# Group 2 of an attention and FFN kernel: all five chunks of the next x turned by DMA, and six weight units split again on the spot

## The chip, the cores and the metric

One core of a Trainium2 chip. The metric is the device time of one execution in microseconds, the median of several runs. TensorE (PE) multiplies, VectorE (DVE), ScalarE (ACT) and GpSimd (POOL) work element by element, and SyncE (SP) mostly issues DMAs.

## The reference

```python
x = A_x                                  # [1, 2048, 640]
xn = layernorm(x)
q, k, v = split(xn @ A_wqkv)             # 32 heads of 20
s = local_attention(q, k, v) @ A_wo      # window of 8 keys, every 2nd row back
g = silu(silu(xn @ B_w1) @ B_w2)         # the FFN: 640 -> 1536 -> 640
out = x + s * g
```

All data are float32.

## The kernel before

**Precision.** A float32 operand is split in a high part (rounded to the fast matmul type by a copy, `hi`) and a low part (value minus high part, `lo`). Each product is three matmuls: high by high, low by high, high by low. So every weight block and every activation needs a high part, made by ScalarE, and a low part, made by VectorE.

**Groups.** The 2048 rows form four groups of 512 (four tiles of 128). For each group the kernel does the QKV product in four quarters of the columns, q = 0 to 3, and then the FFN, while VectorE does the attention. With the FFN of group g goes the output projection (`wo`) of group g - 1, and the preparation of group g + 1's x.

**The FFN's order** (`STEPS`). An "up" unit f makes 128 of the 1536 hidden columns (w1); a "down" unit f multiplies them with 128 rows of w2. In group 2: up 0, five `wo` units, up 1, 2, down 0, 1, 2, up 3, 4, 5, down 3, 4, 5, up 6, 7, 8, down 6, 7, 8, up 9, 10, 11, down 9, 10, 11. After an up unit ScalarE applies SiLU twice (`sh`, the high part, and `sf`, the whole), VectorE subtracts (`sl`). Up units alternate between two PSUM banks (`rot`), `sh` and `sl` have three buffers each, `sf` has one. At the end ScalarE moves the six output banks (`acc`) to G (`gate`).

**Weights.** Each of the units takes the next of seven slots (`w`, numbered 75 to 81 in the rows below), so a slot comes free when the unit seven before is done. A unit met for the first time comes raw over SP's queue into a staging buffer (`xr`, three of them), is split by ScalarE and VectorE, and both halves are stored to memory (`half_w`). Every later time POOL loads the halves, 640 KB, with no splitting.

**The next x.** The normalised rows of group g + 1 stand in XIN. They must be turned: columns become partitions, in five chunks of 128 columns. There are two ways. On TensorE (`split_t`): four transposes into a bank, from which ScalarE writes the high part (`th`) and a whole copy, and VectorE the low part (`tl`). By DMA (`turn_x`): ScalarE separates the 16-bit halves of a chunk into a buffer (`send`, 128x1024), SP issues two DMA transposes, ScalarE puts the halves together again (`join`) and makes the high part, VectorE the low part. The buffers are five pieces of G and TURN, so G must have been read out by the output rows of group g - 1 (`xr<-xr,gate` on POOL) before. Chunks 3 and 4 use as their first buffer what chunks 0 and 1 landed in.

**The order.** All engines but TensorE get their order from a planner (class `Weave`): operations carry a duration and a priority, the planner runs them against its own model of the engines and the DMA, adds dependencies where it sees TensorE wait, and writes them out. `at` is the earliest time of a send or join. Each engine then runs its list in order. A DMA transpose is given 1.27 us a half by size and `SLOW` = 8 us more until it lands; the model knows nothing of a load standing behind a transpose in the queue.

Of the kernel before, what the change touches and what calls it, by code (L numbers as in the profile page):

```python
# [8 lines left out]
F32 = mybir.dt.float32  # L9
# [6 lines left out]
P = 128  # L16
# [7 lines left out]
T = 4  # L24
# [34 lines left out]
O_BACK = (), (80.0, 82.0), (80.0, 82.0), (40.0, 55.0, 60.0)  # L59
X_BY = {1: 2, 3: 0, 4: 1}  # L60
SLOW, ISSUE, SUB_LATE = 8, 2.0, 3
PACE0, PACE = -20.0, 12.0
BACK = {1: 0.0, 2: 40.0}
QAT = 48
OAT = 16
STORE_Q = 1, 3
SHARED = (1, 0), (1, 2), (2, 0), (2, 2), (3, 0)
X_AT = 1.2, 6, 8
# [255 lines left out]
def local_attention_silu_ffn(ctx: ExitStack, tc: tile.TileContext, x, wqkv, wo, w1, w2, out):  # L324
# [152 lines left out]
    def store_at(u):  # L477

        return 1 + (u[0] == "wo" or u[0] == "q" and u[2] in STORE_Q)
# [20 lines left out]
    def raw_tile(k):  # L500
# [7 lines left out]
        return "xr", k % 3  # L508

    def raw_load(k):  # L510
# [12 lines left out]
        pairs = []  # L523
        if u[0] == "q":
            _, q, c = u
            whole = wqkv[c * P:(c + 1) * P, :]
            pairs.append((r.rearrange("p (k m) -> p k m", k=3), whole.rearrange("p (k m) -> p k m", k=3)[:, :, q * CQ:(q + 1) * CQ]))
        elif u[0] == "w1":
            pairs.append((r.rearrange("p (c f) -> p c f", c=DC),
                          w1.rearrange("(c p) f -> p c f", p=P)[:, :, u[1] * P:(u[1] + 1) * P]))  # L530
        else:
            m = wo if u[0] == "wo" else w2
            pairs.append((r, m[u[1] * P:(u[1] + 1) * P, :]))
        by = nc.scalar if k in BY_ACT else nc.sync

        def go():
            for to, frm in pairs:
                by.dma_start(to, frm)
        if k in BY_ACT:
            add("ACT", 0.65 * len(pairs), go, [], kr, -1, nbytes=n * P * 4)  # L540
            return
        dma(go, [], kr, n * P * 4, 1 + k if k < 2 * DC else clock[0] + 5, (0.62 if k < 2 * DC else 0.45) * len(pairs))

    def raws_due(i, k):

        while rawn[0] < len(fresh) and fresh[rawn[0]] <= i + RAW_AHEAD and raw_in.get(raw_tile(rawn[0]), -1) <= k:
            raw_load(rawn[0])
            rawn[0] += 1

    def w_load():  # L550
# [10 lines left out]
        kh, kl = ("wh", s), ("wl", s)  # L561
        due = clock[0]
        if what[i] == "load":
# [16 lines left out]
        if what[i] == "store":  # L580
            kept = dram.tile([P, 2, n], F32, name="half_" + "_".join(map(str, u)))
            halves[u] = kept
            dma(lambda: nc.sync.dma_start(kept, both.bitcast(F32)), [kh, kl], [("half", u)], 2 * n * P * 4, due + 25)
        raws_due(i, k)
# [95 lines left out]
    def turn_x(c, i, by, to, at, back):  # L680
# [3 lines left out]
             (chunk_span("x", c, True), chunk_span("x", c)))  # L684

    def turn_o(c, i, by, to, at, back):
        qs = range(c * P // CQ, ((c + 1) * P - 1) // CQ + 1)
        send(O, c, [("o", q, t) for q in qs for t in (0, 2)], "o", by, to, at)
        join(to, by[0].rearrange("p (t n) -> p t n", t=T), both(by[1]), [], c, i, (OH, OL), back)

    def turn_os(g, i, begun):
# [254 lines left out]
    def qkv_phase(g, i, io):  # L946
        for q in range(NQ):
            if g == 0 and q == 0:
                ps = first_quarter(i)
            else:  # L950
                ps = [bank() for t in range(T)]
                for c in range(DC):
# [12 lines left out]
                    if g:  # L965
                        for k in O_AT.get((q, c), ()):
                            if k not in O_DMA.get(g - 1, ()):
                                o_chunk(g - 1, k, io)
# [212 lines left out]
    def ffn_phase(g, i, ix, io):  # L1181
# [12 lines left out]
        by_dma = X_DMA.get(g, ())  # L1194
        bufs = [("buf", c, h) for c in range(DC) for h in range(2)]
# [29 lines left out]
        if g < NG - 1:  # L1225
            turn_os(g, i, begun)

    add("POOL", 0.7, consts, [], ["consts"], 0)
# [38 lines left out]
```

## Time and profile before

| | |
|---|---|
| median of 3 runs | 598.78 us (598.73 to 599.15) |
| the profiled execution's own time | 598.41 us |
| its span | 596.3 us |
| TensorE clock | 0.999 |
| TensorE busy | 590.6 us, 99% |
| VectorE busy | 513.3 us, 86% |
| ScalarE busy | 248.7 us, 42% |
| POOL busy | 168.2 us, 28% |
| moved by DMA | 164.21 MB, mean 275 GB/s |

Times below are microseconds from the span's start. A row of the timeline gives start, duration, engine, line, operation, output<-input, shape and count, and in brackets the idle time of the engine before it and what ended it. A row of the windows gives the stretch, its length, busy time of PE, PEld (weight load into TensorE), DVE, ACT and POOL with counts, the granted clock, the DMA share and GB/s. A row of groups gives count, then busy time and mean ns, then idle time and what ended it.

### The profile page before, as it was taken

Reading aid. Unit: us, or ns where it says so; the run is one execution under the profiler, and the core shown is the slowest. Engines: PE = TensorE matmul, PEld = TensorE weight load, DVE = VectorE, ACT = ScalarE, POOL = GpSimd, SP = SyncE. Lnnn points to the kernel's source line nnn. Section 1 sums busy time; section 2 is a strip of 40 time slices with the busy share of each in tenths; the row PEclk is TensorE's granted clock in tenths of the full one; section 3 lists DMA queues with packets and bytes.
Section 4 is the critical chain, followed back from the end, with each engine's and each line's share of the span. In section 5 each row is a group of like instructions: output and inputs, shape, how many; then the busy total and the mean of one; then the engine's idle time right before and its main releaser. Section 6 shows DMA issues by size and latency. Waiting matters only on the chain.

```text
span 596.3 us, 9080 instructions
## 1 busy us (share of the span) xinstructions
PE 590.6 (99%) x3443; PEld 555.9 (93%) x3443; DVE 513.3 (86%) x505; ACT 248.7 (42%) x444; POOL 168.2 (28%) x229
## 2 busy tenths in 40 slices
PE   8999999999999999999999999999999999999997
PEld 7999999999999999999999999999999999999997
DVE  6499999999799978999988996999838799998744
ACT  5437375452545223747523604443412333335230
POOL 5800102233110153442221126543121233434100
PEclk9999999999999999999999999999999999999999
DMA  9999999879999999999699999998689999797952
GB/s 295 311 295 334 296 411 402 322 252 300 271 316 326 313 257 324 239 202 239 191 319 306 303 346 304 263 208 286 211 220 283 294 320 295 227 203 215 241 185 89
DMA packets 80263, 164.21 MB, mean 275 GB/s; under 512 B 19949, under 2 KB 44237, under 8 KB 80221
## 3 DMA queue, kind: packets, MB, share of 16 engines
q1 hardware_dynamic: 60381, 83.93, 52.1%
q0 software_dynamic: 19296, 79.31, 46.5%
q8 instruction: 27, 0.44, 0.3%
q10 hardware_dynamic: 544, 0.41, 0.2%
q14 instruction: 15, 0.12, 0.1%
HBM read 107.91 MB, written 34.16 MB: 238 GB/s over the span
## 4 chain that ended last, share of the span: by engine, by line
PE 98%; DMA 0%; DVE 0%; issue 0%
PE acc L1005 23%; PE acc L1007 15%; PE acc L960 10%; PE acc L961 10%; PE acc L962 10%; PE rot L1140 9%; PE rot L1142 9%; PE rot L1141 9%; PE acc L910 2%; PE rot L629 1%; DMA xin<-in_A_x_dram 0%; PE rot L894 0%; PE rot L1123 0%; DVE st L879 0%; PE rot L853 0%; DVE gate L1091 0%
## 5 line engine op out<-in xcount | busy, mean ns | idle before, releaser
L960 PE MATMUL acc<-w,th 128*128 128x480 f32 x300 | 110.6, 369 | 0.0
L961 PE MATMUL acc<-w,tl 128*128 128x480 f32 x300 | 109.8, 366 | 0.0
L962 PE MATMUL acc<-w,th 128*128 128x480 f32 x300 | 109.8, 366 | 0.0
L1005 PE MATMUL acc<-w,sh 128*128 128x384 f32 x384 | 108.6, 328 | 0.0
L1007 PE MATMUL acc<-w,sh 128*128 128x256 f32 x384 | 104.7, 273 | 0.0
L754 DVE TENSOR_TENSOR pr<-q,kv 128x2560 f32<-128x2560 f32 x32 | 90.2, 2819 | 15.9 <-DMA kv<-carry 12.7
L796 DVE TENSOR_TENSOR pr<-q,kv 128x2560 f32<-128x2560 f32 x32 | 91.5, 2860 | 1.4 <-DVE l L757 0.5
L1140 PE MATMUL rot<-th,w 128*128 128x512 f32 x240 | 91.8, 383 | 0.0
L1141 PE MATMUL rot<-tl,w 128*128 128x512 f32 x240 | 91.0, 379 | 0.0
L1142 PE MATMUL rot<-th,w 128*128 128x512 f32 x240 | 91.0, 379 | 0.0
L757 DVE TENSOR_REDUCE l<-pr 128x128 f32<-128x2560 f32 x32 | 89.7, 2804 | 0.2
L1153 ACT ACTIVATE sh<-rot 128x512 fp32r<-128x512 f32 x48 | 28.8, 599 | 134.2 <-PE rot L1142 134.1
L565 POOL DMA_DIRECT2D w<-half_w x72 | 39.0, 542 | 156.6 <-PE acc L1007 57.6
L1007 PEld LDWEIGHTS acc<-w,sh 128*128 128x128 f32 x384 | 73.7, 192 | 0.6
L1005 PEld LDWEIGHTS acc<-w,sh 128*128 128x128 f32 x384 | 72.6, 189 | 0.6
L565 POOL DMA_DIRECT2D w<-half_q x52 | 28.0, 538 | 119.8 <-PE acc L962 74.3
L962 PEld LDWEIGHTS acc<-w,th 128*128 128x128 f32 x300 | 56.7, 189 | 4.0
L960 PEld LDWEIGHTS acc<-w,th 128*128 128x128 f32 x300 | 56.7, 189 | 3.9
L961 PEld LDWEIGHTS acc<-w,tl 128*128 128x128 f32 x300 | 56.7, 189 | 3.9
L1005 PE MATMUL acc<-w,sl 128*128 128x384 f32 x192 | 55.9, 328 | 0.0
L1155 DVE TENSOR_TENSOR sl<-sf,sh 128x512 fp32r<-128x512 f32 x48 | 39.3, 819 | 16.8 <-ACT sf L1154 16.8
L1007 PE MATMUL acc<-w,sl 128*128 128x256 f32 x192 | 52.3, 273 | 0.0
(110 smaller groups left out, 1070.0 us busy)
## 6 DMA issues: line engine op xcount, KB each, us to landing
w<-half_w POOLq DMA_DIRECT2D x72, 640.0 KB, 7.0
w<-half_q POOLq DMA_DIRECT2D x52, 480.0 KB, 5.8
half_w<-w SPq DMA_DIRECT2D x24, 640.0 KB
half_q<-w SPq DMA_DIRECT2D x20, 480.0 KB
kv<-kv SPq DMA_DIRECT2D x15, 560.0 KB
w<-half_wo POOLq DMA_DIRECT2D x10, 640.0 KB, 5.6
kv<-kv SPq DMA_DIRECT2D x15, 420.0 KB
gate<-in_B_w_dram SPq DMA_DIRECT2D x16, 320.0 KB
```

Of the source, the lines that this page charges most:

```text
L565: add("POOL", 1.0, lambda: nc.gpsimd.dma_start(both, src), [("half", u)], [kh, kl], due + 10, nbytes=2 * n * P * 4)
L754: dve(2560, lambda: nc.vector.tensor_tensor(out=PR, in0=win(qq[:, t:t + 2, :], W, 0), in1=win(kv[:, 0, t:t + 2, :], W, CQ), op=OP.mult), h ...
L757: dve(2560, lambda: nc.vector.tensor_reduce(out=l[:, t:t + 2].rearrange("p t w h -> p (t w h)"), in_=PR.rearrange("p t w (h d) -> p (t w h ...
L796: dve(2560, lambda: nc.vector.tensor_tensor(out=PR.rearrange("p t w (h d) -> p t (w h) d", d=DH), in0=e[:, t:t + 2].rearrange("p t w h -> ...
L960: nc.tensor.matmul(o, hi, vh, start=c == 0, stop=False)
L961: nc.tensor.matmul(o, lo, vh, start=False, stop=False)
L962: nc.tensor.matmul(o, hi, vl, start=False, stop=c == DC - 1)
L1005: nc.tensor.matmul(a[t][0][:, :CA].rearrange("p (m h) -> p m h", h=2), st, col_a(w), start=first, stop=last)
L1007: nc.tensor.matmul(b[t // 2][0][:, h * CB:(h + 1) * CB].rearrange("p (m h) -> p m h", h=2), st, col_b(w), start=first and h == 0, stop=las ...
L1140: nc.tensor.matmul(to, wh[:, cs], hi, start=c == 0, stop=False)
L1141: nc.tensor.matmul(to, wh[:, cs], lo, start=False, stop=False)
L1142: nc.tensor.matmul(to, wl[:, cs], hi, start=False, stop=c == DC - 1)
```

## The change

In group 2's FFN, chunks 0 and 1 of group 3's x are turned by DMA too, as 2, 3 and 4 were; the sends are asked for 4, 16, 28, 40 and 52 us after `wo`. In the same FFN the w2 units 6 to 11, which POOL loaded as stored halves, come raw again over SP's queue, at most six units ahead, and are split by ScalarE and VectorE. Their halves from the first group stay stored for groups 1 and 3. The rest of the diff (a helper `raw_ap`, empty tables `O_HOME` and `STORE_W2`, a way to turn group 0's x) does nothing with these tables.

```diff
-X_DMA = {1: (0, 1, 2, 3, 4), 2: (2, 3, 4)}
+X_DMA = {1: (0, 1, 2, 3, 4), 2: (0, 1, 2, 3, 4)}
...
-PACE0, PACE = -20.0, 12.0
+PACE0 = {1: -20.0, 2: 4.0}
+PACE = 12.0
...
+RAW_AGAIN = {("w2", 3): [(f,) for f in range(6, 12)]}
+AGAIN_AHEAD = 6
...
-        what.append("load" if n > at else "store" if n == at and n < again[u] else "split")
+        what.append("load" if n > at and u[1:] not in RAW_AGAIN.get((u[0], n), ()) else "store" if n == at and n < again[u] else "split")
...
+    def ahead(i):
+        return AGAIN_AHEAD if units[i][0] == "w2" and i > fresh[early] else RAW_AHEAD
+
     def raws_due(i, k):
 
-        while rawn[0] < len(fresh) and fresh[rawn[0]] <= i + RAW_AHEAD and raw_in.get(raw_tile(rawn[0]), -1) <= k:
+        while rawn[0] < len(fresh) and fresh[rawn[0]] <= i + ahead(fresh[rawn[0]]) and raw_in.get(raw_tile(rawn[0]), -1) <= k:
...
-                    turn_x(c, ix, by, (piece(G, c), ("buf", c)), clock[0] + PACE0 + PACE * k, clock[0] + BACK[g])
+                    turn_x(c, ix, by, (piece(G, c), ("buf", c)), clock[0] + PACE0[g] + PACE * k, clock[0] + BACK[g])
```

TensorE's list loses two entries of four transposes. The other lists move.

SP's list in group 2's FFN, before: from the first output row of group 1 to the last transposes (`xr` are output rows here).

```order
L1056 DMA out_0_dram<-xr1_108 128x640
L1056 DMA out_0_dram<-xr2_109 128x640
L1056 DMA out_0_dram<-xr0_107 128x640
L662 DMA_TRANSPOSE gate_106<-turn_112 128x4x128 x2
L1053 DMA xr1_108<-in_A_x_dram 128x640
L1056 DMA out_0_dram<-xr1_108 128x640
L662 DMA_TRANSPOSE gate_106<-gate_106 128x4x128 x4
```

SP's list at the same place, after, from the first transposes on (`xr<-in_B_w2` are raw rows of units 6 to 11, in this order).

```order
L676 DMA_TRANSPOSE gate_106<-turn_112 128x4x128 x2
L1090 DMA out_0_dram<-xr0_107 128x640
L1087 DMA xr1_108<-in_A_x_dram 128x640
L545 DMA xr2_109<-in_B_w2_dram 128x640
L676 DMA_TRANSPOSE gate_106<-gate_106 128x4x128 x2
L545 DMA xr0_107<-in_B_w2_dram 128x640
L1090 DMA out_0_dram<-xr1_108 128x640
L545 DMA xr1_108<-in_B_w2_dram 128x640
L545 DMA xr2_109<-in_B_w2_dram 128x640
L676 DMA_TRANSPOSE gate_106<-turn_112 128x4x128 x2
L545 DMA xr0_107<-in_B_w2_dram 128x640
L676 DMA_TRANSPOSE gate_106<-gate_106 128x4x128 x2
```

Behind the last of these follow the raw rows of unit 11 (`xr1_108`) and chunk 4's two transposes. Five pairs of transposes now alternate with the raw rows, one queue for all.

ScalarE's list, before, from up unit 8's activations (`sh2_86`) to up unit 10's (`sh1_85`).

```order
L1153 ACTIVATE sh2_86<-rot1_120 128x512
L1154 ACTIVATE sf_110<-rot1_120 128x512
L670 ACTIVATE xin_105<-gate_106 128x2x4x128
L676 ACTIVATE th1_70<-xin_105 128x512
L670 ACTIVATE xin_105<-gate_106 128x2x4x128
L676 ACTIVATE th1_70<-xin_105 128x512
L1153 ACTIVATE sh0_84<-rot0_119 128x512
L1154 ACTIVATE sf_110<-rot0_119 128x512
L1153 ACTIVATE sh1_85<-rot1_120 128x512
```

ScalarE's list, after, over the same stretch: `w2_77`, `w6_81`, `w0_75` and `w1_76` are the high parts of units 8, 9, 10 and 11, the two `gate<-xin` the sends of chunks 3 and 4, and the join is chunk 2's.

```order
L1187 ACTIVATE sh2_86<-rot1_120 128x512
L671 ACTIVATE gate_106<-xin_105 128x1024
L590 ACTIVATE w2_77<-xr1_108 128x640
L671 ACTIVATE gate_106<-xin_105 128x1024
L590 ACTIVATE w6_81<-xr2_109 128x640
L1188 ACTIVATE sf_110<-rot1_120 128x512
L590 ACTIVATE w0_75<-xr0_107 128x640
L684 ACTIVATE xin_105<-gate_106 128x2x4x128
L690 ACTIVATE th1_70<-xin_105 128x512
L590 ACTIVATE w1_76<-xr1_108 128x640
L1187 ACTIVATE sh0_84<-rot0_119 128x512
L1188 ACTIVATE sf_110<-rot0_119 128x512
```

The high part of unit 11 now stands ahead of up unit 9's activations (`sh0_84`, `sf_110`).

VectorE's list in group 3, before, around the gate products that empty the banks of group 2's `wo`.

```order
L796 TENSOR_TENSOR pr_102<-q1_98,kv1_94 128x2560
L1040 TENSOR_TENSOR gate_106<-acc4_117,gate_106 128x2x192
L1040 TENSOR_TENSOR gate_106<-acc5_118,gate_106 128x2x192
L1040 TENSOR_TENSOR gate_106<-acc2_115,gate_106 128x4x128
L1040 TENSOR_TENSOR gate_106<-acc0_113,gate_106 128x2x192
L1040 TENSOR_TENSOR gate_106<-acc1_114,gate_106 128x2x192
L1040 TENSOR_TENSOR gate_106<-acc3_116,gate_106 128x4x128
L802 TENSOR_TENSOR kv1_94<-pr_102 128x1280
```

VectorE's list there, after.

```order
L830 TENSOR_TENSOR pr_102<-q1_98,kv1_94 128x2560
L836 TENSOR_TENSOR kv1_94<-pr_102 128x1280
L788 TENSOR_TENSOR pr_102<-q2_99,kv2_95 128x2560
L1074 TENSOR_TENSOR gate_106<-acc4_117,gate_106 128x2x192
L1074 TENSOR_TENSOR gate_106<-acc5_118,gate_106 128x2x192
L1074 TENSOR_TENSOR gate_106<-acc2_115,gate_106 128x4x128
L1074 TENSOR_TENSOR gate_106<-acc0_113,gate_106 128x2x192
L1074 TENSOR_TENSOR gate_106<-acc1_114,gate_106 128x2x192
L1074 TENSOR_TENSOR gate_106<-acc3_116,gate_106 128x4x128
```

An addition and a multiply of the attention now stand ahead of the gate products.

More of the change, by code (lines that the diff above doesn't have):

```diff
@@ L477, in store_at @@
     def store_at(u):
[L479 removed]
+        return 1 + (u[0] == "wo" or u[0] == "q" and u[2] in STORE_Q or u[0] == "w2" and u[1] in STORE_W2)
     for u in units:
@@ L522, in raw_load @@
         raws[i] = r, kr
[L523 to L533, printed above, removed]
+        pairs = [raw_ap(u, r)]
         by = nc.scalar if k in BY_ACT else nc.sync
@@ L562, in w_load, with keep @@
         due = clock[0]
+        def keep():
+            kept = dram.tile([P, 2, n], F32, name="half_" + "_".join(map(str, u)))
+            halves[u] = kept
+            dma(lambda: nc.sync.dma_start(kept, both.bitcast(F32)), [kh, kl], [("half", u)], 2 * n * P * 4, due + 25)
         if what[i] == "load":
@@ L580, in w_load @@
         if what[i] == "store":
-            kept = dram.tile([P, 2, n], F32, name="half_" + "_".join(map(str, u)))
-            halves[u] = kept
-            dma(lambda: nc.sync.dma_start(kept, both.bitcast(F32)), [kh, kl], [("half", u)], 2 * n * P * 4, due + 25)
+            keep()
         raws_due(i, k)
@@ L689, in turn_o, with turn_home @@
         join(to, by[0].rearrange("p (t n) -> p t n", t=T), both(by[1]), [], c, i, (OH, OL), back)
+    def turn_home(g, i):
+        todo = O_HOME.get(g, {})
+        if not todo:
+            return
+        old = [("xin", t) for t in range(T)]
+        place = [(piece(XIN, k), ("xp", k)) for k in range(DC)] + [(TURN, ("turn",))]
+        new = [k for _, p in place[:DC] for k in both(p)]
+        free_for(old, new)
+        for n, (c, at) in enumerate(todo.items()):
+            turn_o(c, i, place[2 * n], place[2 * n + 1], clock[0] + at, clock[0] + at + HOME_BACK)
+        free_for(new, old)
     def turn_os(g, i, begun):
@@ L1194, in ffn_phase @@
         by_dma = X_DMA.get(g, ())
-        bufs = [("buf", c, h) for c in range(DC) for h in range(2)]
+        bufs = [("buf", c, h) for c in range(DC) for h in range(2)] if g else []
+        if not g:
+            for k, c in enumerate(by_dma):
+                turn_first(c, ix, begun + X0_OUT + X0_PACE * k, begun + X0_BACK + X0_PACE * k)
         for kind, f in plan(g):
```

20 lines of the change are left out of this document (19 added, 1 removed).

## The prediction

> **What bounds the kernel now.** I read the page's engine shares first, then the chain that ended last, then TensorE's own waits, and only then the stage that is changed.
>
> ```profile
> PE 590.6 (99%) x3443; PEld 555.9 (93%) x3443; DVE 513.3 (86%) x505; ACT 248.7 (42%) x444; POOL 168.2 (28%) x229
> PE 98%; DMA 0%; DVE 0%; issue 0%
> PE rot L866 <- POOL ident masks.py:199: 1.4, 1, 1.4
> PE rot L894 <- DVE xin L884: 0.5, 1, 0.5
> ```
>
> TensorE carries 98% of the chain, and its list of waits has these two rows only, both in the first microseconds. From then to the last product it never waits, so a TensorE instruction taken out saves its slot, and every wait that the change brings to TensorE costs in full. The windows cover the second half of group 2 (its FFN ends near 429.5) and group 3's first products:
>
> ```profile
> 346.00:418.00 72.00, 72.00 (x439) 67.79 (x438) 66.15 (x50) 27.04 (x38) 32.41 (x41) 1.00 1.08 281
> 418.00:490.00 72.00, 72.00 (x403) 67.90 (x402) 53.82 (x41) 23.66 (x53) 16.38 (x29) 1.00 0.97 264
> ```
>
> TensorE is busy 72.00 of 72 us at clock 1.00, VectorE 66.15, ScalarE 27.04, and the DMA share is full (1.08). VectorE has room only behind the FFN.
>
> **TensorE's side: the gain.** Four transposes of 128x128 go, twice. Around the first:
>
> ```profile
> 366.48 0.27 PE L1007 MATMUL acc<-w,sl 128*128 128x256 f32 x1
> 366.59 0.60 PE L629 MATMUL rot<-ident,xin 128*128 128x128 f32 x4
> 366.94 0.41 PE L1005 MATMUL acc<-w,sh 128*128 128x384 f32 x1
> 367.19 0.27 PE L1007 MATMUL acc<-w,sh 128*128 128x256 f32 x1
> 367.30 0.33 PE L1005 MATMUL acc<-w,sh 128*128 128x384 f32 x1
> ```
>
> The record of 0.60 overlaps the next one, so I go by starts. In the steady stream a 256-column product starts and the next 384-column one follows 0.11 later (367.19 to 367.30). Here the 384-column product's partner starts at 367.19, where without transposes it would start 0.17 after 366.59: 0.43 us for the four. Twice that is 0.86 us. A page of the Trainium skill speaks for more: "TensorE: Matmul & The Clock Gate", Part 4, gives about 275 ns for one transpose in a kernel's context, by which eight would be 2.2 us. The rows' 0.11 us each decides.
>
> **The other engines: six more splits, two more turned chunks.**
>
> ```profile
> L574 ACT ACTIVATE w<-xr 128x640 fp32r<-128x640 f32 x18 | 13.1, 739 | 2.2 <-PE acc L962 1.7 <-DMA half_w<-w 0.5
> L578 DVE TENSOR_TENSOR w<-xr,w 128x640 fp32r<-128x640 f32 x18 | 14.6, 819 | 1.7 <-ACT w L574 1.3 <-DMA half_q<-w 0.5
> L633 ACT ACTIVATE th<-rot 128x512 fp32r<-128x512 f32 x20 | 11.9, 595 | 39.0 <-PE rot L629 39.0
> L657 ACT ACTIVATE gate<-xin 128x1024 uint16<-128x1024 uint16 x5 | 5.3, 1051 | 3.3 <-POOL xr L1054 3.3
> 450.06 2.83 DVE L754 TENSOR_TENSOR pr<-q,kv 128x2560 f32<-128x2560 f32 x1 [12.68 <-DMA kv<-carry]
> ```
>
> VectorE gets six subtractions of 0.82, 4.9 us; the low parts of chunks 0 and 1 stay, at the same price. With 66.15 of 72 us busy it falls behind by about that, but it stands idle 12.68 us before 450.06, so the delay ends there; were that gap gone, group 3's attention would start late. ScalarE pays 6 x 0.74 for the high parts and, for each of two chunks, a send (1.05), a join (1.36) and a high part (0.63) in place of two evictions of 0.60: 4.4 + 3.7 = 8.1 us, hidden in 45 idle ones unless the order makes it wait. POOL loses six issues of 0.53. The memory queues lose 6 x 640 KB and gain 6 x 320 KB raw and four transposes. None of this touches TensorE's sum; only a wait can.
>
> **Where a wait could reach TensorE.** The raw rows go into three buffers on SP's queue, between transposes, and ScalarE takes them in a fixed order: a late one holds what stands behind it. What a load behind transposes costs:
>
> ```profile
> 366.79 3.50 SPq L662 DMA_TRANSPOSE gate<-turn  x2
> 370.39 0.53 SPq L1053 DMA_DIRECT2D xr<-in_A_x_dram  x1
> 382.62 2.97 POOL L1054 TENSOR_TENSOR xr<-xr,gate 128x640 f32<-128x640 f32 x1 [1.60 <-DMA xr<-in_A_x_dram]
> 498.18 2.69 SPq L662 DMA_TRANSPOSE kv<-kv  x2
> 501.00:505.00 4.00, 4.00 (x21) 3.49 (x20) 4.00 (x7) 1.09 (x2) 0.00 (x0) 1.00 1.27 98
> 505.00:508.00 3.00, 3.00 (x20) 2.81 (x19) 3.00 (x3) 1.09 (x2) 1.07 (x2) 1.00 1.43 212
> 508.00:510.00 2.00, 2.00 (x16) 2.00 (x16) 2.00 (x3) 0.00 (x0) 0.57 (x1) 1.00 0.95 358
> ```
>
> The x row issued at 370.39 behind a pair of transposes let POOL go at 382.62: 12.2 us, beside many weight loads. The pair issued at 498.18, with little else on the queues, drains by about 508: the rate is back at 358 GB/s, after 98 and 212. So it drains between 505 and 508, 7 to 10 us after its first issue.
>
> I call the raw rows of the second product's unit f "raw f", and the first product's unit f "up f". Most waits have room. SP now issues chunk 0's pair ahead of the third output store, some 2 us earlier (364.7), so what stands right behind it, raw 6 too, lands near 381. Raw 7 waits for that store to land and stands behind chunk 1's pair: another 7 us, 388. On ScalarE its high part holds chunk 0's join, which nobody needs before 428, and up 6's activations, which must be through before up 8 uses the same bank, near 396: 4 us to spare after join and activations. Raw 8, 9 and 10 are issued before chunk 3's pair. The narrow place is raw 11: it is issued behind chunk 3's pair, and on ScalarE its high part stands ahead of up unit 9's two activations. Rows of before:
>
> ```profile
> 393.77 0.60 ACT L1153 ACTIVATE sh<-rot 128x512 fp32r<-128x512 f32 x1 [6.80 <-PE rot L1142]
> 394.87 1.28 ACT L774 ACT_TABLE_LOAD   x1
> 396.17 0.42 ACT L774 ACTIVATE q<-l 128x256 f32<-128x256 f32 x1
> 401.82 1.36 ACT L670 ACTIVATE xin<-gate 128x1024 uint16<-128x1024 uint16 x1
> 403.21 0.63 ACT L676 ACTIVATE th<-xin 128x512 fp32r<-128x512 f32 x1
> 413.35 0.60 ACT L1153 ACTIVATE sh<-rot 128x512 fp32r<-128x512 f32 x1 [7.59 <-PE rot L1142]
> 416.59 0.60 ACT L1153 ACTIVATE sh<-rot 128x512 fp32r<-128x512 f32 x1 [2.14 <-PE rot L1142]
> ```
>
> *Deadline.* TensorE finishes up 9 at 413.35 and up 10 at 416.59; 0.86 earlier after the change, so up 11 wants to start at 415.7. It writes the bank that up 9 used, and waits until both activations (1.1 together, 393.77 to 394.87) have read it. Raw 11's high part (0.74) goes first, so raw 11 must land by 415.7 - 1.1 - 0.74 = 413.9.
>
> *Landing.* ScalarE takes up 6 at 392.9 (393.77 - 0.86). In the new order follow its second activation and chunk 1's join (1.1 + 2.0), up 7 (1.1), two table loads and the exponential (3.0) and up 8 (0.6): 400.7. Then it sends chunk 3, 1.05 us, and SP issues the pair from 401.8 to 404.5-405.3, and raw 11 behind it (its buffer is free by then: VectorE subtracts raw 8 near 404). The lower end is the quiet pair: drained 7 to 10 us after 401.8, then 320 KB, 0.9 us at the row's 358 GB/s: 409.7 to 412.7. The upper end is the x row: 405.3 + 12.2 = 417.5. I take 412.3, next to the quiet row, since here POOL's weight loads of units 9 and 10 are gone from the queues. So 1.6 us remain and TensorE doesn't wait; at the upper end it waits 417.5 - 413.9 = 3.6 us.
>
> On this the pages differ with the trace. "Advanced Engine Details and Errata", X-Bar Transpose (TRN2), says transposes run as fast as other copies, 350 to 400 GB/s. By that a pair would be gone in under 1 us (an estimate), raw 11 would land near 407, and this wait couldn't arise. The trace, with 98 GB/s over 501 to 505, disagrees.
>
> *VectorE in the same place.* It subtracts raw 11 ahead of the small parts of up 9, 10 and 11.
>
> ```profile
> 429.50 0.37 PE L960 MATMUL acc<-w,th 128*128 128x480 f32 x1
> ```
>
> At 429.50 the FFN is over. Its last unit is twelve pairs of a 384- and a 256-column product, 0.28 each, and the first small part is in the third pair, 2.8 us before the end: 429.5 - 0.86 - 2.8 = 425.8. If VectorE stands until raw 11's high part is there, 413.1, then come its subtraction (0.8), chunk 2's low part and up 9's small part (0.6 each), an addition (1.4), a multiply (2.8), up 10's (0.6), a sum (2.8) and up 11's (0.6): 423.3. Some 2.5 us to spare.
>
> *Group 3.* The planner now puts an addition (1.4) and a multiply (2.7) ahead of the six gate products that empty the banks:
>
> ```profile
> 485.51 2.82 DVE L796 TENSOR_TENSOR pr<-q,kv 128x2560 f32<-128x2560 f32 x1 [0.46 <-DVE l L757]
> 500.84 3.14 DVE L1040 TENSOR_TENSOR gate<-acc,gate 128x384 f32<-128x384 f32 x6
> 506.46 0.33 PE L1005 MATMUL acc<-w,sh 128*128 128x384 f32 x1
> ```
>
> They would start at 500.84 - 0.86 + 4.1 = 504.1 and end at 507.2. The second product starts at 506.46 - 0.86 = 505.6 and comes to the last bank after four pairs and a half, 1.3 us later: 506.9. So TensorE waits 0.3, or not at all if the wait of 0.46 before 485.51 goes, for whose cover the order now has a maximum ahead. I take nothing.
>
> **The sum.** Profiled execution: 598.41 (span 596.3 and 2.1 around it) - 0.86 + 0 = 597.55. The median shown is 598.78, 0.37 above, so 597.9 on it, 0.14% less. About 0.2% (1.2 us) is what a measurement of this kernel can tell from no change, so this counts as the same.
>
> **Rivals.**
> - *Raw 11 lands as late as the x row did* (slower). Price: 3.6 us of TensorE's wait, 598.78 - 0.86 + 3.6 = 601.5. It decides from a landing of 416.0 on, where the wait (2.1) exceeds 0.86 + 1.2. For it: the row at 370.39. Against: the queues are emptier. 0.14.
> - *Small waits eat the gain* (the change does nothing): raw 11 between 414 and 416, or the low parts of units 8 and 11 late by a microsecond after VectorE's 4.9 us more. 0.3 to 2.0 us: 598.2 to 599.9. 0.25.
> - *Group 3's banks are emptied late*: 0.3 us, 598.2. 0.09.
> - *Transposes cost their whole record*: 0.60 and 0.08 more on the product behind (0.41 against 0.33), twice, 1.36 us: 597.4, faster by 0.23%. The starts speak against it. The page's 275 ns would make it 596.6. 0.05.
>
> **How the numbers follow.** The forecast has 0.47: 597.9, own range 597.6 to 598.2. Its companions without a visible difference (0.25, 0.09) make "same" 0.81; faster 0.05; slower 0.14. The range from 597.4 to 600.0 leaves out the late landing.
>
> **What the changed profile would show.** If right: TensorE's waits still only at the start, 8 transposes fewer, the low parts of w in six more rows, VectorE's gap before group 3 near 8 us. If wrong: a TensorE wait on ScalarE's up activation near 415, behind a ScalarE wait for the raw row; or on the gate products near 506. The forecast fails most easily if a pair of transposes takes longer there than the quiet one did.

## The result and the profile after

| | before | after |
|---|---|---|
| median | 598.75 us (20 runs) | 603.7 us (20 runs) |
| lowest and highest | 598.42, 600.85 | 599.42, 613.55 |
| runs above 600 us | 3 of 20 | 17 of 20 |
| ratio of the undisturbed runs | | 1.0073, 95% interval 1.0047 to 1.0098 |

The change is slower by 0.7%; the medians differ by 4.95 us. (The ratio leaves out runs more than 1.5% above the fastest; here such runs are the effect itself, so medians and counts stand beside it.) The forecast was 597.9 and its range ended at 600.0. Even the best run is above the forecast, and the runs now lie 14 us apart. The profiled execution is a short one, 599.91 us. The page's busy times and its chain's shares by engine, answering to the first lines shown of before:

```profile
PE 590.4 (99%) x3435; PEld 555.5 (93%) x3435; DVE 519.0 (87%) x511; ACT 252.5 (42%) x450; POOL 162.8 (27%) x223
PE 93%; DVE 2%; DMA 2%; issue 1%; ACT 1%; SPq 0%; DVEq 0%; ACTq 0%
```

TensorE's list of waits has a new first row, and the windows show where it falls: in the second stretch TensorE is busy 70.14 of 72 us.

```profile
PE rot L1174 <- DVE tl L653: 1.9, 1, 1.9
PE rot L900 <- POOL ident masks.py:199: 1.4, 1, 1.4
PE rot L928 <- DVE xin L918: 0.3, 1, 0.3
```

```profile
346.00:418.00 72.00, 72.00 (x436) 67.68 (x435) 64.62 (x51) 31.30 (x43) 27.45 (x32) 1.00 0.98 253
418.00:490.00 72.00, 70.14 (x390) 65.91 (x389) 62.22 (x47) 23.38 (x55) 19.46 (x32) 1.00 1.03 265
```

The evacuation `gate<-acc` opens at the end of each FFN, so the distance between two of these rows measures a stage. Group 1's and group 2's, before and then after:

```profile
281.55 0.49 ACT L1224 ACTIVATE gate<-acc 128x384 f32<-128x384 f32 x1 [1.84 <-PE acc L1005]
427.12 0.49 ACT L1224 ACTIVATE gate<-acc 128x384 f32<-128x384 f32 x1 [1.48 <-PE acc L1005]
```

```profile
281.64 0.49 ACT L1261 ACTIVATE gate<-acc 128x384 f32<-128x384 f32 x1 [1.84 <-PE acc L1039]
426.34 0.49 ACT L1261 ACTIVATE gate<-acc 128x384 f32<-128x384 f32 x1 [4.29 <-PE acc L1039]
```

Group 2's stage went from 145.57 to 144.70 us: a gain of 0.87, where 0.86 was forecast, is there in this execution. By the same rows group 3's stage (427.12 to 573.57 before, 426.34 to 574.92 after) went from 146.45 to 148.58. So in a short run 0.87 is won in group 2 and 2.13 lost in group 3. What makes the other runs up to 14 us longer this profile doesn't show. The kernel before has long runs too, but few: of its 154 runs, here and beside the experiments, 7 were above 602 us (of the change's 20 here, 13). The stages serve for all runs below:

| stage length, us | group 2 | group 3 |
|---|---|---|
| before | 145.57 | 146.45 |
| the change, four executions (599.91, 599.86, 599.86, 601.42 us) | 144.70, 144.70, 145.89, 146.80 | 148.58, 148.45, 147.29, 147.85 |

### The profile page after: what moved, and what is told of

Read it like the earlier page. It is cut to its first block, busy times and chain, and to the rows that moved or that the text cites. A ratio compares the mean times of both kernels' runs of the same rounds, so it can differ in the third digit from the quotient of the medians.

```text
span 598.1 us, 9080 instructions
## 1 busy us (share of the span) xinstructions
PE 590.4 (99%) x3435; PEld 555.5 (93%) x3435; DVE 519.0 (87%) x511; ACT 252.5 (42%) x450; POOL 162.8 (27%) x223
## 4 chain that ended last, share of the span: by engine, by line
PE 93%; DVE 2%; DMA 2%; issue 1%; ACT 1%; SPq 0%; DVEq 0%; ACTq 0%
PE acc L1039 22%; PE acc L1041 15%; PE rot L1174 9%; PE acc L994 9%; PE acc L996 9%; PE acc L995 9%; PE rot L1175 9%; PE rot L1176 9%; PE acc L944 2%; DMA kv<-kv 2%; PE rot L643 1%; DVE pr L788 1%; DMA xin<-in_A_x_dram 1%; DVE pr L830 0%; PE rot L928 0%
## 5 line engine op out<-in xcount | busy, mean ns | idle before, releaser
L581 POOL DMA_DIRECT2D w<-half_w x66 | 35.7, 541 | 155.2 <-PE acc L1041 61.8
L1189 DVE TENSOR_TENSOR sl<-sf,sh 128x512 fp32r<-128x512 f32 x48 | 41.2, 858 | 18.2 <-ACT sf L1188 18.1
L1174 PEld LDWEIGHTS rot<-th,w 128*128 128x128 f32 x240 | 45.4, 189 | 7.8 <-DVE tl L653 2.1
```

Source lines behind the costliest of these rows:

```text
L1174: nc.tensor.matmul(to, wh[:, cs], hi, start=c == 0, stop=False)
```

## The experiments

### Which part costs

Theory A: group 3's new order on VectorE and SyncE. Theory B: raw loads late behind the transposes of group 2's FFN. Theory C: the further transposes themselves.

**Turn alone.**

```diff
-RAW_AGAIN = {("w2", 3): [(f,) for f in range(6, 12)]}
+RAW_AGAIN = {}
```

> Turn alone: all five chunks of x by DMA, units 6 to 11 of the second product's weights still loaded as stored halves. In group 3 this kernel's instructions stand nearly as in the kernel before. Theory A (the loss comes from the new order in group 3: the 112-partition halo copy of quarter 1 issued last, VectorE's low part of chunk 3 of the attention's output behind a product): 597.9 us, 0.86 below the kernel before, and runs that agree within 1 us. Theory B (raw loads behind the transposes of FFN 2 arrive late in most runs): the raw loads are gone, so 597.9 as well, but the last stored halves may wait. Theory C (any further DMA transposes delay the transfers of group 3): 600 to 604, scattered like the changed kernel.

Measured: median 602.64 (597.65 to 614.92, 9 of 12 runs above 600), before 598.7. The best run has the whole gain, yet the scatter is there without any raw unit. Neither A nor B alone holds. The profiled execution (602.57) lost its time in group 2. The timeline rows of SyncE, and of GpSimd and VectorE, which hang on it, and then a row of TensorE's waits (total, times, longest):

```profile
363.79 4.42 SPq L676 DMA_TRANSPOSE gate<-turn  x2
370.33 1.39 SPq L1087 DMA_DIRECT2D xr<-in_A_x_dram  x1
371.82 14.29 SPq L676 DMA_TRANSPOSE gate<-gate  x2
389.05 1.54 POOL L1088 TENSOR_TENSOR xr<-xr,gate 128x640 f32<-128x640 f32 x1 [11.79 <-DMA xr<-in_A_x_dram]
391.90 4.16 DVE L830 TENSOR_TENSOR pr<-q,kv 128x2560 f32<-128x2560 f32 x1 [5.94 <-POOL mark L857]
```

```profile
PE acc L1039 <- DVE sl L1189: 2.9, 3, 1.2
```

The second pair goes out 8 us behind the first and holds SyncE for 14.29 us (the quiet pair shown of before took 2.69). The x row between the two took 18.7 us (370.33 to 389.05) instead of 12.2. GpSimd waited for it with its marker behind (`mark`, which VectorE's next product waits for), VectorE for the marker, TensorE 2.9 us for VectorE. That the second pair alone makes the x row late isn't shown: it took 12.7 us in the profile after, which has the early pair, and 21.3 and 19.4 us in two kernels below (the whole change with chunk 1's pair behind the store, and the best version) that issue the pair only after 389.

**Raw alone.**

```diff
-X_DMA = {1: (0, 1, 2, 3, 4), 2: (0, 1, 2, 3, 4)}
+X_DMA = {1: (0, 1, 2, 3, 4), 2: (2, 3, 4)}
...
-PACE0 = {1: -20.0, 2: 4.0}
+PACE0 = {1: -20.0, 2: -20.0}
```

> Raw alone: units 6 to 11 of the second product's weights come raw and are split, chunks 0 and 1 of x are turned by TensorE as before. In group 3 this kernel's instructions stand as in the changed kernel. Theory A (new order in group 3): as slow and as scattered as the changed kernel plus the two turns by TensorE, 600 to 605 us, with TensorE waiting for VectorE in the first product of FFN 3. Theory B (raw loads late behind the transposes): no pair of transposes stands ahead of units 6 to 9 any more than before, 598.5 to 599.5. Theory C (further transposes): 598.5 to 599.

Measured: 600.2 (598.98 to 603.01); ratio 1.0022 (1.0000 to 1.0044). Its group 3 stage is 147.57, 1.12 above before's.

**The change with group 3's old sequence.** `FIXED` holds each queue's list, for group 3 that of the kernel before; the planner's tries are left out.

```diff
-                    c = can[e]
+                    c = [o for o in can[e] if o.seq == turn[e][0]]
...
-                can[e].remove(o)
+                can[e].remove((o, turn[e].pop(0))[0])
...
-        for o in self.plan():
+        for o in self.order():
```

> The changed kernel, with the instructions of group 3 on VectorE, ScalarE, GpSimd and SyncE in the sequence of the kernel before; everything up to the start of group 3 stands as in the changed kernel. Theory A (new order in group 3): 597.9 us, runs within 1 us, no TensorE wait in group 3. Theory B (raw loads late behind the transposes in FFN 2) and theory C (further transposes): unchanged at 600 to 604, scattered.

Measured: 602.05 (597.97 to 611.32, 9 of 12 above 600). Group 3's stage is 146.45, as before, and the lowest run fell from 599.42 to 597.97: theory A is right for 1 to 2 us and explains none of the scatter. The profiled execution was the longest of its runs (611.32). It first lost 8.0 us in group 1's FFN (that stage took 153.47 us, in the profile after 145.51), which the change doesn't touch and where five pairs stood before as well, and then this in group 2 (SyncE, GpSimd, TensorE; its times there are 8 to 10 us later than in the profile after):

```profile
378.28 7.98 SPq L676 DMA_TRANSPOSE gate<-gate  x2
382.25 1.15 POOL L581 DMA_DIRECT2D w<-half_w  x2
401.26 0.48 PE L1174 MATMUL rot<-th,w 128*128 128x512 f32 x1 [2.35 <-DMA w<-half_w]
```

The halves of up 7, issued beside the second pair, landed 19 us later; TensorE waited 2.35.

**The change again**, no edit.

> The changed kernel once more, for a second look at where its time goes: 599.4 to 613 us. Theory A: what is above 599.4 is TensorE waiting for VectorE in group 3 (quarters 1 to 3 and the first products of FFN 3). Theory B: it is TensorE waiting in FFN 2 (about 390 to 430 us) for weights of units 7 to 11 or for the split before them.

Measured: 599.86. TensorE waited 0.6 for `tl` in group 3, as A has it, and 0.56 in group 2 for ScalarE's `sf`, which no theory had named.

**Raw alone with group 3's old sequence** (the same edit as above).

> Raw alone, with group 3 in the sequence of the kernel before: tells what the raw units cost by themselves, and by the difference to raw alone (600.2 us) what the new order of group 3 costs. Theory A in its small form (the new order of group 3 costs 1 to 2 us): 598.7 us, equal to the kernel before. Rival G (the raw loads and the six further splits cost it, in FFN 2): 599.5 to 600.5, as with raw alone.

Measured: 599.0 (598.49 to 613.59, 3 of 12 above 600; ratio 1.0013, 0.9999 to 1.0026), 1.2 below raw alone; its group 3 stage is 146.45. So in the median the raw units cost next to nothing and group 3's order about 1.2 here. The profiled execution was the longest (613.59), and 13.5 us of that were lost in group 1's FFN, with no transpose added anywhere.

### Where the second pair stands

Theory D: the second pair close behind the first is what costs. Rival E: any two more pairs. H: the last pair lands late.

**Turn alone, chunk 1's pair behind the store of the last x row**, old group 3; **the whole change with the same edit.**

```diff
+        stored.append(wv.ops[-1])
...
+                    n = len(wv.ops)
                     turn_x(c, ix, by, (piece(G, c), ("buf", c)), clock[0] + PACE0[g] + PACE * k, clock[0] + BACK[g])
+                    for o in wv.ops[n:] if (g, c) == (2, 1) else ():
+                        if o.eng == "SP":
+                            wv.chain(stored[-1], o)
```

> Turn alone, but the pair of transposes for chunk 1 stands on SyncE behind the store of the last residual row, so that the row's load has only chunk 0's pair ahead of it, as before; group 3 in the sequence of the kernel before. Theory D (two pairs close together hold up the x row behind them, GpSimd waits for that row with the loads of weights and the halves of the value products queued behind it, and TensorE waits for VectorE or for weights): 597.9 us, and runs scattered no more than those of the kernel before (598.1 to 600). Rival E (any two further pairs in FFN 2 load the transfer engines, wherever they stand): median 601 to 603, runs to 612, as with the turn alone.

> The whole change, with chunk 1's pair behind the store of the last residual row and group 3 in the sequence of the kernel before. Theory D: 597.9 us, scattered no more than the kernel before, 0.9 below it. Rival E (any two further pairs in FFN 2): median 601 to 603. Rival F (raw units behind the later pairs, which now stand closer together from 388 us on): single runs of 600 to 605 with TensorE waiting at 400 to 425 us.

Measured: 601.53 (7 of 12 above 600) and 598.16 (3 of 12 above 600). In the whole change the scatter nearly goes, as D says; in the turn alone it stays. There the stored halves, 640 KB each, still come all through the FFN, and behind the store the second pair and the third stand on end: from 379.6 on they held SyncE 22 us. But that profiled execution is a short one (598.11) in which TensorE doesn't wait, so what costs in the long runs of the turn alone isn't shown. It is only shown that the pair's place isn't all.

The whole change's profiled execution (600.80) still lost 2.9 us in group 2, and not as F has it. The late load is raw 6, which has chunk 0's pair alone ahead of it (SyncE, ScalarE, TensorE):

```profile
373.02 0.33 SPq L545 DMA_DIRECT2D xr<-in_B_w_dram  x1
392.74 0.74 ACT L590 ACTIVATE w<-xr 128x640 fp32r<-128x640 f32 x1 [11.66 <-DMA xr<-in_B_w_dram]
398.07 0.48 PE L1176 MATMUL rot<-th,w 128*128 128x512 f32 x1 [1.21 <-ACT sf L1190]
```

It landed 19.7 us after its issue, though chunk 1's pair goes out only at 392.28. ScalarE then splits raw 7, at 394.40, and TensorE waits 1.21 for the activations behind. So a load can be that late behind a single pair.

**Turn alone, GpSimd's last addition later** (GpSimd's list; `half_w2_8` is the next load).

```diff
 L581 DMA w6_81<-half_w1_8_149 128x1280
-L1088 TENSOR_TENSOR xr1_108<-xr1_108,gate_106 128x640
...
 L843 TENSOR_TENSOR o_101<-kv1_94 128x2x160
+L1088 TENSOR_TENSOR xr1_108<-xr1_108,gate_106 128x640
 L581 DMA w2_77<-half_w2_8_154 128x1280
```

> Turn alone, with one edit: GpSimd adds the last residual row behind the next marker and the next halves of a value product and behind one more load of weights, so that it does not wait for the row with that work behind it; the transposes stand as in the turn alone. Theory D1 (GpSimd's wait for the row is what passes the delay on): median 598 to 599, few runs over 601. Theory D2 (the weights' own transfers are held up by the two pairs): as scattered as the turn alone, median about 602.

Measured: 605.58 in 4 runs, none below 605.0. Both predictions missed. With the row's store, and the later pairs behind it, put off to 390, chunk 4's pair came last:

```profile
430.21 1.34 ACT L684 ACTIVATE xin<-gate 128x1024 uint16<-128x1024 uint16 x1 [6.24 <-DMA gate<-gate]
433.42 0.77 PE L994 MATMUL acc<-w,th 128*128 128x480 f32 x1 [4.76 <-ACT gate L1261]
```

The join of chunk 4 waits for its landing; the gate's evacuations stand behind it, since they write over the place; group 3's first product waits 4.76 us for them.

**The kernel before with a late last pair.**

```diff
-clock[0] + PACE0 + PACE * k, clock[0] + BACK[g])
+clock[0] + (50.0 if (g, c) == (2, 4) else PACE0 + PACE * k), clock[0] + BACK[g])
```

> The kernel before, with its last pair of transposes (chunk 4) held back: it is sent at about 403 us instead of 389, nothing else is turned by DMA, and group 3 keeps its sequence. Theory H (a pair lands 10 to 21 us after its issue, by chance; the join of the last chunk stands on ScalarE ahead of the gate's evacuations at 426 us, which write over the place where it landed, so a pair issued after about 405 us makes TensorE wait at the start of group 3 in part of the runs, and its granted clock falls behind that): lowest 598.4, but a third or more of the runs above 600, up to 610. Rival E (two further pairs load the transfer engines): no pair is added, so like the kernel before, 598.7 and hardly a run above 600.

Measured: 598.76 (598.28 to 600.87): no more scatter than before. Issuing one lone pair 14 us later costs nothing. It doesn't refute H, though: in the profiled execution chunk 4's join ran at 420.70 without waiting, 6.3 us before the evacuations (427.02), so the pair wasn't late enough to hold them. H's path is real: it costs 4.76 us in the experiment before this one, and it stands in group 1's FFN in the three executions that lost most there. The one without any added transpose, raw alone with group 3's old sequence (ScalarE; then TensorE's list of waits):

```profile
293.74 1.34 ACT L684 ACTIVATE xin<-gate 128x1024 uint16<-128x1024 uint16 x1 [8.95 <-DMA gate<-gate]
```

```profile
PE acc L994 <- ACT gate L1261: 6.4, 1, 6.4
```

In the other two, the change with group 3's old sequence and the one with GpSimd's addition later, TensorE waits 5.9 and 9.6 us in the same place.

**The change with chunk 4 in a place of its own; the same with chunk 1's pair behind the store.** Both with group 3's old sequence.

```diff
+                    own = OWN.get((g, c))
+                    by, to = (spare(0, 0), spare(0, 1)) if own else (by, (piece(G, c), ("buf", c)))
...
-                    turn_x(c, ix, by, (piece(G, c), ("buf", c)), clock[0] + PACE0[g] + PACE * k, clock[0] + BACK[g])
+                    turn_x(c, ix, by, to, clock[0] + PACE0[g] + PACE * k, clock[0] + (own or BACK[g]))
```

> The change with group 3 in the sequence of the kernel before, and chunk 4 turned through the keys' and values' tile of quarter 0 instead of the gate's tile, so that its join can stand behind the gate's evacuations on ScalarE (needed by TensorE at 438 us instead of 426). To be compared with the same without that (602.05 us, 9 of 12 runs above 600). Theory H (late landing of the last pair): median 598 to 598.5, few runs above 600. Theory D (the first two pairs close together, the x row behind them, GpSimd's wait): as scattered as without it, median about 602. If both hold, between them.

> Both edits on the change: chunk 1's pair behind the store of the last residual row, chunk 4 turned through the tile of quarter 0 with its join behind the gate's evacuations, group 3 in the sequence of the kernel before. To be compared with the first edit alone (598.16 us, 4 of 12 runs above 599). Theories D and H together: 597.8 to 597.9, at most one run in ten above 599.5, so 0.8 below the kernel before. If neither is the cause: 598.2 to 602, still scattered.

Measured: 601.16 (7 of 12 above 600), and 597.93 (597.58 to 598.35, all 12 below 598.4), ratio to before 0.997 (0.9942 to 0.9997). The first edit takes H's path out of group 2, and the scatter stays, so there H isn't what makes it. Again it is the second pair's place that decides. The latter is the best version and beats both kernels. Its loads aren't fast: raw 6 took 19.7 us there too (370.38 to 390.06), but raw 7, issued ahead of the second pair, follows at 391.93. Whether chunk 4's own place adds to 598.16 with 3 of 12 above 600, twelve runs can't tell.

**The kernel before with two pairs close together** (SyncE's list).

```diff
 L1053 DMA xr1_108<-in_A_x_dram 128x640
+L662 DMA_TRANSPOSE gate_106<-gate_106 128x4x128 x2
 L1056 DMA out_0_dram<-xr1_108 128x640
-L662 DMA_TRANSPOSE gate_106<-gate_106 128x4x128 x4
+L662 DMA_TRANSPOSE gate_106<-gate_106 128x4x128 x2
```

> The kernel before, with one edit: chunk 3's pair of transposes is issued right behind the load of the last residual row (about 371 us) instead of behind that row's store (386 us). Three pairs as before, nothing raw. Theory D (a second pair that close behind the first, at 363 to 378 us, is what costs): median 600 to 603, runs to 610. Rival E (it takes five pairs): like the kernel before, 598.6.

Measured: 599.82 (598.47 to 614.77, 6 of 12 above 600; before 598.74, 5 of 23). With three pairs and nothing else changed, long runs come more often: 4 of 12 are above 602 us, before 1 of 23 beside it and 7 of 154 in all. So it doesn't take five pairs, and E falls as it was put; the ratio, 1.0025 (0.9997 to 1.0053), still takes in no change. The second pair held SyncE for 16.26 us, and TensorE waited 0.7 for stored halves:

```profile
366.08 3.02 SPq L662 DMA_TRANSPOSE gate<-turn  x2
369.20 0.54 SPq L1053 DMA_DIRECT2D xr<-in_A_x_dram  x1
369.82 16.26 SPq L662 DMA_TRANSPOSE gate<-gate  x2
```

D is half shown: the pair now stands nearer to the first and also goes out 16 us earlier, amid the stores, the x row and the stored halves, and no run parts the two. Standing close isn't enough by itself, since the kernel before has two pairs on end later, without harm:

```profile
386.06 5.59 SPq L662 DMA_TRANSPOSE gate<-gate  x4
```

### By what path

D1: GpSimd's wait for the x row. D2: stored halves. J: raw 7, whose load stands behind the second pair.

**The change, two further executions**, no edit.

> The changed kernel again, for a profile of a long execution (two thirds of its runs are above 601 us). Theory D1: what is above 599.4 is lost between 385 and 430 us, and begins with GpSimd waiting over 8 us for the last residual row. Theory D2: it begins with TensorE waiting for a stored half of a unit that was issued between 365 and 385 us.

> As the look before it: theory D1, a loss that begins with GpSimd's wait for the last residual row; theory D2, one that begins with a late stored half; theory H, one at 426 to 435 us that begins with the join of chunk 4.

Measured: 601.42 and 599.86. The 1.56 us between them, with a path that D1, D2 and H hadn't named (SyncE, ScalarE and TensorE, first of the longer, then SyncE and ScalarE of the shorter):

```profile
372.17 5.98 SPq L676 DMA_TRANSPOSE gate<-gate  x2
379.32 0.34 SPq L545 DMA_DIRECT2D xr<-in_B_w_dram  x1
394.12 0.74 ACT L590 ACTIVATE w<-xr 128x640 fp32r<-128x640 f32 x1 [7.32 <-DMA xr<-in_B_w_dram]
397.16 0.59 ACT L1188 ACTIVATE sf<-rot 128x512 f32<-128x512 f32 x1
397.80 0.48 PE L1174 MATMUL rot<-th,w 128*128 128x512 f32 x1 [1.48 <-ACT sf L1188]
```

```profile
370.27 10.13 SPq L676 DMA_TRANSPOSE gate<-gate  x2
380.44 0.57 SPq L545 DMA_DIRECT2D xr<-in_B_w_dram  x1
388.46 0.74 ACT L590 ACTIVATE w<-xr 128x640 fp32r<-128x640 f32 x1 [3.17 <-DMA xr<-in_B_w_dram]
```

Raw 7 landed 14.8 us after its issue in one and 8.0 in the other. ScalarE splits it ahead of chunk 0's join and up 6's activations, and up 8 needs the bank that these empty. From the split's start to up 8's it is 397.80 - 394.12 = 3.68 us, and without the wait up 8 would have started at 396.32; so the deadline is 392.64: a raw 7 that comes later delays up 8 by as much. At 388.46 TensorE doesn't wait. In the profile after raw 7 came less than 1 us before it:

```profile
391.76 0.74 ACT L590 ACTIVATE w<-xr 128x640 fp32r<-128x640 f32 x1 [5.92 <-DMA xr<-in_B_w_dram]
```

**GpSimd's last addition later, in the change with group 3's old sequence** (GpSimd's list).

```diff
 L581 DMA w6_81<-half_w1_8_149 128x1280
-L1088 TENSOR_TENSOR xr1_108<-xr1_108,gate_106 128x640
 L857 TENSOR_TENSOR mark_111<-pr_102 128x1
 L841 TENSOR_TENSOR kv1_94<-kv1_94 128x2x320
 L843 TENSOR_TENSOR o_101<-kv1_94 128x2x160
+L1088 TENSOR_TENSOR xr1_108<-xr1_108,gate_106 128x640
```

> The change with group 3 in the sequence of the kernel before, and GpSimd's addition of the last residual row behind the next marker and halves of a value product. To be compared with the same without that edit (602.05 us, 9 of 12 runs above 600). Theory D1 (GpSimd's wait passes the delay on to VectorE): median 598 to 599. Theory D2 (stored halves land late by themselves): as before, about 602.

Measured: 603.22 (10 of 13 above 600): D1 is out for the change. The profiled execution, again the longest (618.58; it lost 12.4 us in group 1's FFN, so its times are some 13 us later), shows the path at full size:

```profile
386.47 14.62 SPq L676 DMA_TRANSPOSE gate<-gate  x2
401.14 0.58 SPq L545 DMA_DIRECT2D xr<-in_B_w_dram  x1
410.96 0.74 ACT L590 ACTIVATE w<-xr 128x640 fp32r<-128x640 f32 x1 [3.23 <-DMA xr<-in_B_w_dram]
414.62 0.79 PE L1174 MATMUL rot<-th,w 128*128 128x512 f32 x1 [5.14 <-ACT sf L1188]
```

The pair holds SyncE 14.62 us, raw 7 goes out only then, and 3.66 us after its landing TensorE starts up 8, having waited 5.14. Raw 6, ahead of the pair, took 20.0 us (386.05 to 406.03) and alone would have put raw 7's split at about 407.7, 1.9 us past the deadline here (414.62 - 5.14 - 3.68 = 405.80), an estimate.

**Raw 7 ahead of the second pair**, in the change with group 3's old sequence (SyncE's list).

```diff
 L545 DMA xr2_109<-in_B_w2_dram 128x640
+L545 DMA xr0_107<-in_B_w2_dram 128x640
 L676 DMA_TRANSPOSE gate_106<-gate_106 128x4x128 x2
-L545 DMA xr0_107<-in_B_w2_dram 128x640
```

> The change with group 3 in the sequence of the kernel before, and one edit: the load of raw unit 7 stands on SyncE ahead of chunk 1's pair of transposes, not behind it (the pair itself then goes out 3 to 5 us later). To be compared with the same without that edit (602.05 us, 9 of 12 runs above 600). Theory J (raw 7 lands after 392.5 us, ScalarE waits for it with the activations of the up products behind, TensorE waits for those, as much as it lands later): raw 7 lands before 390, median 597.9 to 598.5, few runs above 600. Theory D2 (the early pair delays stored halves or other loads just as much): median 600 to 602, TensorE waiting elsewhere between 385 and 425 us.

Measured: 598.17 (10 of 12 below 598.7, two above 600; the kernel before beside it 598.85); without the edit 602.05 (before beside it 598.7). With one load moved past one pair the median is 3.9 us lower.

```profile
370.95 8.90 SPq L545 DMA_DIRECT2D xr<-in_B_w_dram  x2
379.90 3.42 SPq L676 DMA_TRANSPOSE gate<-gate  x2
384.44 0.75 ACT L590 ACTIVATE w<-xr 128x640 fp32r<-128x640 f32 x1 [3.02 <-DMA xr<-in_B_w_dram]
386.64 0.74 ACT L590 ACTIVATE w<-xr 128x640 fp32r<-128x640 f32 x1 [0.52 <-DMA xr<-in_B_w_dram]
```

Raw 7 lands at 386.64, 6 us early. But the pair, too, goes out 10 us later than in the profile after, at 379.90, and takes SyncE 3.42 us only; so the edit may also help the stored halves, and doesn't separate the two.

**Raw 7 behind the second pair in the best version** (SyncE's list).

```diff
-L545 DMA xr0_107<-in_B_w2_dram 128x640
 L1090 DMA out_0_dram<-xr1_108 128x640
 L676 DMA_TRANSPOSE gate_106<-gate_106 128x4x128 x2
+L545 DMA xr0_107<-in_B_w2_dram 128x640
```

> The best version (597.93 us, 12 of 12 runs below 598.4) with one edit: the load of raw unit 7 stands on SyncE behind chunk 1's pair, so that it is issued at about 392 us instead of 385. Theory J: it lands at 396 to 399 us, 4 to 6 us after 392.5, TensorE waits that long for ScalarE at about 392 us, and its granted clock falls behind the wait (it was 0.57 for 3.5 us behind a wait of 2.4 us): 603 to 608 us in nearly every run. If raw 7 does not carry the loss: 598 to 599.

Measured: 598.42, with 4 of 12 above 600 (up to 610.36) where the best version had none. The direction is J's, the size isn't: in the profiled execution raw 7 came at 392.51, 3 us after its issue at about 389.4, just at the deadline; this pair took SyncE 2.55 us only. What the four long runs lost isn't shown.

## Why the prediction was wrong

- **The gain was right.** 8 transposes are worth 0.87 us (145.57 to 144.70); 0.86 was forecast. The figure of the Trainium skill ("TensorE: Matmul & The Clock Gate", Part 4, about 275 ns) would have made it 2.2, an estimate; the stages bear out 0.11 a transpose.
- **The step that failed: raw 7.** It reads "another 7 us, 388", with "4 us to spare after join and activations". The bank's deadline was right (392.64 by the rows above; the prediction's 396 less its split, join and activations is 392.2). The landing was mis-sized: 388.46, 391.76 and 394.12 in three executions of the change, 8 to 15 us after the load's own issue. Raw 6, on which the 388 builds, was put at 381 and came at 383.61, 384.15 and 385.11. I had sized a load behind chunk 1's pair by the quiet pair at 498.18, though that pair is the second within 7 us, amid x rows, stores and stored halves; there pairs held SyncE for 5 to 16 us and the loads beside them took up to 20. I spent the upper bound, the x row's 12.2, on raw 11 alone. With it raw 7 would have stood at 381 + 12.2 = 393, past its deadline.
- **Raw 11 was no narrow place.** It landed at 408.8, not 412.3; behind chunk 3's pair the queues had room, as I had argued (DMA share 0.59 over 405 to 408 us). The rival that was to decide had the right mechanism and the wrong unit.
- **Group 3: one order row too few.** I costed the gate products (they started at 504.62, no wait, as forecast) and not the halo copies (`kv<-kv`, the neighbouring rows' keys and values that SyncE copies) and the low part `tl` that the planner also moved. Rows of VectorE in group 3, after, and then the last one's counterpart before:

```profile
467.49 2.83 DVE L788 TENSOR_TENSOR pr<-q,kv 128x2560 f32<-128x2560 f32 x1 [0.49 <-DMA kv<-kv]
473.08 0.68 DVE L653 TENSOR_TENSOR tl<-rot,th 128x512 fp32r<-128x512 f32 x1
478.06 2.82 DVE L788 TENSOR_TENSOR pr<-q,kv 128x2560 f32<-128x2560 f32 x1
480.80 0.68 DVE L653 TENSOR_TENSOR tl<-rot,th 128x512 fp32r<-128x512 f32 x1
```

```profile
476.78 0.68 DVE L639 TENSOR_TENSOR tl<-rot,th 128x512 fp32r<-128x512 f32 x1
```

  TensorE's up 0 needs the bank that the row at 480.80 frees, 4 us later than before, and waits 1.9 for it. With before's sequence the stage is back at 146.45. The term was 0 and measured 0.8 to 2.1.
- **VectorE's cover held.** The gap before group 3 is 6.90 us; 8 was forecast. But group 3's attention starts at 451.52, not 0.86 before 450.06: it waits for a halo copy.
- **The sum.** In medians: 603.7 to 602.05 goes with group 3's order, 602.05 to 598.17 with the order of raw 7 and the early pair, and 598.17 and 597.93 are near the 597.9 that I had forecast for the whole. Medians of runs that scatter by 14 us are rough; the stages' 0.8 to 2.1 is the firmer figure for group 3.

Shown is that the order of chunk 1's pair and the loads around it makes most of the long runs of the change. With group 3's old sequence and the pair early, 26 of 37 runs in three experiments are above 600 us; with the pair held back or raw 7 ahead of it, 9 of 48 in four. In the kernel before, a pair moved forward brings some. Shown, too, is one path: a raw load that comes to ScalarE after the deadline makes TensorE wait, raw 7 for 1.5 and 5.1 us in two executions, raw 6 for 1.2 in one; a stored half cost 2.35 in one. What the best version has is not faster loads but a raw 7 issued sooner, which comes 0.7 us before the deadline.

Not settled is why a load takes 8 us once and 20 another time, and how much of the runs above 602 us is raw loads and how much stored halves, as the change's own profiles are all of short runs. Nor is the share of group 1's FFN: three profiled executions, each the longest of its kernel, lost 8.0, 12.4 and 13.5 us there, more than half of what they are above the shortest run of their kernel. TensorE's largest wait in each is H's, behind a last pair that lands late; why it lands late is open, and as one of the three has no added transpose, the longest runs can't all be put down to group 2's FFN.

## What to carry to other kernels

Of a load that is moved behind a DMA transpose, take the landing from the busiest row there is, not from a quiet one, leave room beyond it (the x row's 12.2 us became 21.3), and put it against the deadline of whatever stands behind it on an in-order engine: an engine that is 58% idle still stalls TensorE when it waits for one load ahead of an activation. Space transposes in the queue by their landing, not by the time that a planner asks for, and put urgent loads ahead of them. When a planner reorders a later stage as a by-product, compare that stage's list row by row, or fix its order.

## What the runs showed of the hardware

**The granted clock falls behind short waits.** Windows of three executions, each of what follows a wait (stretch, length, busy times of PE, PEld, DVE, ACT, POOL, clock, DMA share, GB/s): the longer of the change's two further executions, with a wait of 1.48 us, the change with group 3's old sequence, 2.35, and the one with GpSimd's addition later, 5.14.

```profile
397.80:400.00 2.20, 2.20 (x10) 1.96 (x11) 2.20 (x4) 2.17 (x3) 0.00 (x0) 1.00 0.96 290
```

```profile
401.30:405.00 3.70, 3.70 (x10) 2.96 (x11) 0.00 (x0) 0.17 (x1) 0.00 (x0) 0.59 0.48 178
```

```profile
414.60:418.00 3.40, 3.38 (x8) 2.75 (x9) 3.40 (x4) 3.35 (x5) 0.00 (x0) 0.50 1.62 352
418.00:421.00 3.00, 3.00 (x16) 2.66 (x16) 2.97 (x5) 2.96 (x4) 2.04 (x2) 0.87 0.62 164
```

The clock stays at 1.00 behind 1.48 us (to 403 too), is 0.59 for 3.7 us behind 2.35 (0.50 from 402 to 405), and 0.50, then 0.87, behind 5.14: a wait of 2.35 costs about 1.5 us more, an estimate ((1 - 0.59) x 3.7). The Trainium skill, "TensorE: Matmul & The Clock Gate", Part 1, has the clock fall to half after an idle window of about 3.4 us. Here half came after a shorter wait.

**Behind a pair of transposes in traffic** the queues are full and little is moved. Over 385 to 390 us of the profile after, some 7 us after the second pair left SyncE, all engines' share is 1.30 at 55 GB/s. SyncE's queue alone takes 1.25 of it, and 378 of the 430 packets are under 512 bytes; that these are the transposes' is inferred:

```profile
385.00:390.00 5.00, 5.00 (x38) 4.95 (x37) 5.00 (x3) 0.84 (x1) 1.28 (x2) 1.00 1.30 55
```
